# Attention, SwiGLU gate and output projection on one core: another place for the divided feed-forward tile, and another rule for the order of score copies

## The chip, the core and the metric

The kernel runs on one core of a Trainium2 chip. The time is device microseconds of one execution; the figure for a kernel is the median of several. A profiled execution also has a span, from its first to its last instruction, which is a little shorter than its time. The engines are PE (TensorE, matrix products), DVE (VectorE), ACT (ScalarE), POOL (GpSimd) and SP (which here only issues DMAs). They run side by side, each in the order of its own instructions, and wait for one another by semaphores.

## What is computed

One layer on a sequence of 2048 tokens of width 512, in fp32: a layer norm, full attention with 32 heads of 16, a SwiGLU feed-forward of width 1792 whose output gates the attention's output, and a residual.

```python
def _A_ref(x, wqkv, wo):                      # B, S, D = 1, 2048, 512; H = 32; Dh = 16
    q, k, v = ...                             # x @ wqkv, by heads
    scores = jnp.einsum("bhqd,bhkd->bhqk", q, k) * scale
    p = _softmax(scores, axis=-1)
    o = jnp.einsum("bhqk,bhkd->bhqd", p, v)
    return ... @ wo

def _B_ref(x, w_gate, w_up, w_down):          # F = 1792
    g = _silu(x @ w_gate)
    u = x @ w_up
    return (g * u) @ w_down

xn = _layernorm(x, axis=-1)
s = _A_ref(xn, A_wqkv, A_wo)
g = _silu(_B_ref(xn, B_w_gate, B_w_up, B_w_down))
return x + s * g
```

## The kernel before

**Two kinds of work side by side.** After a first stage (layer norm, projections) comes one long stage in which attention and feed-forward are mixed by hand. Nothing is scheduled by the compiler (`manual_schedule`): the order of the Python calls is the order on each engine.

**Attention** is cut into 32 *units*: eight groups of four heads by four stretches of 512 queries. A unit goes through 16 key tiles of 128 keys, in three *blocks* (96 in all; here they are counted from 0, so unit u has blocks 3u to 3u+2). `blocks` holds unit, first key tile and number n of key tiles; `run` issues one block. Each key tile gives two *pairs* of heads. For a pair, PE makes two score products of 128 by 512 at once, one in the upper and one in the lower 64 rows of its array, and ACT takes the exponential of both.

- A **direct pair** (`"D"`, function `scored`) uses one of two PSUM score tiles in turn; ACT reads it straight from PSUM (L954). The next but one direct pair needs that exponential done.
- A **copied pair** goes through a single spare PSUM bank (`acc[1]`) in two *halves*: `"A"` makes the first product and DVE copies it to SBUF (L1010), `"B"` the second (L1016). Each half needs the copy before it done, since there is only one bank. ACT takes the exponentials of the copied pairs at the end of the block (L1024). A half uses only one half of the array's rows; `lower` turns the order of the next products round, so that the other half of the rows is not idle.

After a block's scores come its **value products** (`values`, L409): per key tile four products in four column strips of the array, written as two instructions each, 8 instructions per key tile in all. They need the exponentials.

**Feed-forward** is a stream of *products* (`"F"`, one call of `fill(1)`; `both`, L187): two matrix products at once, into the PSUM tiles bankx (upper rows) and banky (lower rows). For each of four token blocks and two groups of seven feature tiles there are seven *gate and up tiles* of 24 products each and then four *down tiles* of 21 products each. At the end of a gate and up tile ACT takes a tanh (L239) and DVE makes two products (L240, L241) and two splits into high and low parts; at the end of a down tile DVE adds both banks to an accumulator. Work for DVE that may come later is put into `chores`, with a cost in units of a product, and `run` places chores between copies where `events` leaves room; `tidy` places all that is left.

**How they are matched.** `sizes` holds the number of products for each block: normally one tile per block. There are 87 tiles left at the start and 88 blocks before the tail (`early = 88`), so one tile must be divided over two blocks. Blocks 88 to 95 take the products of the output projection (18, 24, 24, 24, 12, 12, 24, 24; L380, `project_out`), which halfway through each tile turns the two banks round after DVE has read one element of each (`turned_over`, L384).

- A unit normally has n of 5, 5 and 6, with the 6 where a block has most products. Units with a divided tile have 6, 6, 4 and then 4, 6, 6, so that the blocks with half a tile have 4 key tiles.
- `begins` lists blocks whose first two direct pairs are made early: `begin` issues them in the block before, ahead of that block's last key tile of value products. In `events` such a block has `ahead` set to 2.
- `events(n, f, ahead)` sets the order within a block. It gives each direct pair and each copied half a time in units of a product (direct pairs at 0, 1 and then from 7 on some 4 to 5 apart, halves from 2.2 on some 5.6 to 8 apart), sorts them, and fills the room with products. Where the times are crowded they are issued in the order of the list, as close as they come.

From the names in `order`'s rows: acc_80 is `acc[0]` (value products), acc_81 the spare bank, score_8970 and score_8971 the two score tiles.

Of the kernel before, what the change touches and what calls it, by code (L numbers as in the profile page):

```python
# [21 lines left out]
D = 512  # L22
H = 32
DH = 16
F = 1792
# [14 lines left out]
DC = D // HALF  # L40
# [3 lines left out]
EPS = 1e-5  # L44
TURNS = (0, 0, 0, 0, 0, 2, 4, 6, 8, 10, 13, 16, 16)
COPIES = ((0, 0, 0, 1, 1, 1, 1, 0, 0, 0, 0, 2), (1, 1, 0, 0, 1, 1, 1, 1, 2, 2, 0, 0))
QSLOT = (0, 1, 0)
KSLOT = (0, 0, 1)

# [2 lines left out]
def tile_block(ctx: ExitStack, tc: tile.TileContext, x, wqkv, wo, w_gate, w_up, w_down, out):  # L52
    nc = tc.nc
    ctx.enter_context(tc.manual_schedule())
    x, out = x[0], out[0]
# [39 lines left out]
    def load_rows(dst, src, slots):  # L95
        for h in range(2):
            for s, part in enumerate(slots):
                r = h * HALF + 2 + s * DH
                sp.dma_start(dst[r:r + DH].bitcast(F32),
                             src[part].rearrange("(j h d) t -> h d j t", j=2, h=2)[h])  # L100
# [5 lines left out]
    def load_q(u, i=None):  # L106
        g, b = divmod(u, NB)
        load_rows(qst[u % 2 if i is None else i], q_d[:, g * 64:(g + 1) * 64, b * TB:(b + 1) * TB], QSLOT)

# [353 lines left out]
    units = NG * NB  # L463
# [19 lines left out]
    sizes = []  # L483
    for _ in range(NB):
        for part in GROUPS:
            nf = part.stop - part.start
            sizes += [3 * DC] * nf + [3 * nf] * NT
    split = sizes[-1] // 2
    sizes = sizes[1:-1] + [sizes[-1] - split, split]
    early = len(sizes)  # L490
    pair = 6 * DT
    sizes += [6 * (DT - 1), pair, pair, pair, pair // 2, pair // 2, pair, pair]
    begins = (early - 2, early - 1, early, early + 4, early + 5)

    blocks, opened = [], []
    for u in range(units):
        opened.append(len(blocks))
        if u == 0:
            ns = [4, 6, 6]
        elif u >= units - 4:  # L500
            ns = ([4, 6, 6] if u % 2 else [6, 6, 4])
        else:
            ns = [5] * 3
            far = sizes[len(blocks):len(blocks) + 3]
            ns[far.index(max(far)) if far[1] < max(far) else 1] = 6
        kt = 0
        for n in ns:
            blocks.append((u, kt, n))
            kt += n

    def events(n, f, ahead):
        length = 2 * n - ahead + f
        need = 2 * n - max(2, (10 * length + 46) // 40)
        fit = (10 * length + 55) // 112
        copied = n - 3 if ahead else max(0, min(need, fit)) if now else 0
        direct = 2 * n - copied
        gap = max(4, min(5, (length - 8) / max(1, direct - 2)))
        marks = [] if ahead else [(0, "D"), (1, "D")]
        marks += [((0.5 if ahead else 7) + gap * i, "D") for i in range(direct - 2)]
        marks += [((0.3 if ahead else 2.2) + max(5.6, min(8, (length - 5) / (2 * copied))) * i, "AB"[i % 2]) for i in range(2 * copied)]  # L520
        marks.sort(key=lambda mark: mark[0] - 0.6 * (mark[1] == "D"))
        out = []
        at = left = 0
        for t, kind in marks:
            while left < f - (kind != "D") and at < t:
                out.append((at, "F"))
                left += 1
                at += 1
            out.append((at, kind))
            at += 1 if kind == "D" else 0.5  # L530
        return direct, out + [(at + i, "F") for i in range(f - left)]

    with ExitStack() as pro:
        pc = pro.enter_context(tc.tile_pool(name="pc", bufs=1))
# [118 lines left out]
        def split_x(b, t, av, between=None):  # L653
            hi, lo = (xt[b % 2][j][:, :, t * P:(t + 1) * P] for j in range(2))
            nc.scalar.copy(hi, av)
            if between:
                between()
            dve.tensor_sub(lo, av, hi.bitcast(F32))
# [119 lines left out]
        def copy_fx(i):  # L778
            i, w = divmod(i, 2)
            i, u = divmod(i, 2)  # L780
            j, h = divmod(i, 2)
            dst = fx[halves[h], j].rearrange("p (c u) t -> u p c t", u=2)[u]
            nc.scalar.copy(dst[:, 2 * w:2 * w + 2], xt[0][j][halves[u], 2 * w:2 * w + 2])

        copied = list(range(16))
# [11 lines left out]
        for b in range(NB):  # L797
# [3 lines left out]
            for n, (make, i) in enumerate(slots):  # L801
# [27 lines left out]
                if b == 0 and n == 2:  # L829
                    split_x(0, 0, xf)  # L830
                for _ in range(COPIES[b][n] if b < 2 else 0):
                    copy_fx(copied.pop(0))
# [57 lines left out]
        with tc.If(fast < 1):  # L890
            with tc.tile_pool(name="gen", bufs=1) as gen:
                for h in range(2):
                    pool.memset(qst[0][h * HALF:h * HALF + 2].bitcast(F32), 0.0)
                for g in range(NG):
                    for b in range(NB):
                        u = g * NB + b
                        load_q(u, 0)
                        mx = gen.tile([P, 4 * NT, 4], F32, tag="mx", name="mx")
                        for j in range(NB):
                            load_k(g, j, j % 2)  # L900
                            for i in range(4 * NT):
                                h, t = divmod(i, NT)
# [60 lines left out]
    def run(u, first, n):  # L963
        nonlocal lower
        f = sizes.pop(0) if sizes else 0
        direct, todo = events(n, f, len(begun))
        if now == 0:
            for _ in range(4):
# [172 lines left out]
```

## Time and profile before

| | |
|---|---|
| time, median of 3 runs | 1397.09 us (1396.32 to 1397.9) |
| time of the profiled execution | 1397.09 us |
| its span | 1395.3 us, granted TensorE clock 0.999 |
| value products (L409) | 4096 instructions |
| direct pairs (L954) | 860 exponentials |
| copied pairs (L1010, L1016, L1024) | 164 |
| DVE busy | 755.9 us of the span |

The main view is the chain of work that ended last, in order of time. It follows the program back from its last instruction, at each step to what released it or to the instruction before it on its engine. A row gives start, length and the work. In the long stage nearly all of it is PE, so a block can be read off between two of its runs of value products: a row `x40` is the value products of a block with 5 key tiles, `x48` of one with 6, `x32` of one with 4; where the next block is begun early the last key tile has a row `x8` of its own. The end of such a run (start plus length) is the end of the block.

The other views used are the timeline (instructions of an engine in order of time, with the wait ahead of them in brackets and its releaser) and the page's tables of engines and of groups of instructions.

### The profile page before, as it was taken

What the parts mean: (1) busy time and instruction counts of PE and PEld (TensorE: products, weight loads), DVE (VectorE), ACT (ScalarE), POOL (GpSimd) and SP (SyncE); (2) the same over time, 40 slices, a digit from 0 to 9 for tenths busy, and PEclk for the clock granted to TensorE, in tenths of its full rate; (3) what the DMA queues carried; (4) which work ended last, traced back from release to release, by engine and by line L of the source; (5) the groups of instructions that cost most, each with busy time, mean ns of one, the idle gap of its engine ahead of it and who ended that gap; (6) DMA issues with size and microseconds to landing.
All of it is one profiled execution on the core that took longest, in us unless ns stands there. A gap on an engine that the chain in (4) does not pass through costs nothing.

```text
span 1395.3 us, 27643 instructions
## 1 busy us (share of the span) xinstructions
PE 1387.7 (99%) x11193; PEld 849.8 (61%) x11193; DVE 755.9 (54%) x1293; ACT 1087.4 (78%) x1245; POOL 73.7 (5%) x92
## 2 busy tenths in 40 slices
PE   9999999999999999999999999999999999999998
PEld 7777755655665565565556556655655665564555
DVE  6674555455645653556456645654565445555544
ACT  6753678877888877787888778778877877889785
POOL 4200200000000000000000000000000000000222
PEclk9999999999999999999999999999999999999999
DMA  7778641043534511154514303256134113234323
GB/s 228 271 246 267 173 107 43 14 115 85 130 86 118 119 43 36 51 132 97 136 53 110 97 13 73 74 141 149 57 76 114 32 47 80 63 92 141 116 86 137
DMA packets 126953, 148.13 MB, mean 106 GB/s; under 512 B 12524, under 2 KB 79340, under 8 KB 126052
## 3 DMA queue, kind: packets, MB, share of 16 engines
q1 hardware_dynamic: 121620, 125.79, 34.8%
q0 software_dynamic: 4912, 20.12, 3.9%
q8 instruction: 89, 1.46, 0.4%
q14 instruction: 44, 0.36, 0.1%
q10 hardware_dynamic: 288, 0.39, 0.1%
HBM read 106.68 MB, written 39.58 MB: 105 GB/s over the span
## 4 chain that ended last, share of the span: by engine, by line
PE 88%; ACT 0%; DVE 0%; issue 0%; DVEq 0%
PE acc L409 32%; PE bankx L187 23%; PE score L948 17%; PE banky L187 10%; PE acc L948 3%; PE bankx L380 2%; PE banky L380 1%; ACT pr L954 0%; PE acc L1078 0%; PE bankx L1078 0%; PE score L1078 0%; DVE pr L1010 0%; DVE y L1085 0%; DVE pr L1016 0%; DVE fx L1022 0%
## 5 line engine op out<-in xcount | busy, mean ns | idle before, releaser
L954 ACT ACTIVATE pr<-score 128x1024 f32<-128x1024 f32 x860 | 813.4, 1032 | 226.2 <-PE score L948 224.5
L409 PE MATMUL acc<-pr,vst 128*17 128x512 f32 x4096 | 459.1, 593 | 0.0
L948 PE MATMUL score<-qst,kst 50*128 50x512 f32 x1720 | 395.4, 412 | 0.1
L187 PE MATMUL bankx<-fx,guh 64*128 64x512 f32 x896 | 333.5, 393 | 0.1
L187 PE MATMUL banky<-fx,guh 64*128 64x512 f32 x896 | 324.9, 393 | 0.0
L409 PEld LDWEIGHTS acc<-pr,vst 128*17 128x17 f32 x4096 | 109.9, 97 | 290.6 <-issue 270.9
L948 PEld LDWEIGHTS score<-qst,kst 50*128 50x128 f32 x1720 | 176.3, 184 | 142.5 <-issue 66.3
L1010 DVE COPY pr<-acc 128x512 f32<-128x512 f32 x164 | 113.3, 691 | 188.1 <-PE acc L948 186.0
L187 PE MATMUL bankx<-wd,hh 64*128 64x512 f32 x672 | 201.2, 392 | 0.0
L187 PE MATMUL banky<-wd,hh 64*128 64x512 f32 x672 | 198.8, 393 | 0.0
L187 PEld LDWEIGHTS bankx<-fx,guh 64*128 64x128 f32 x896 | 166.6, 186 | 18.4 <-issue 0.9
L187 PE MATMUL banky<-fx,gul 64*128 64x512 f32 x448 | 175.6, 392 | 0.0
L187 PE MATMUL bankx<-fx,gul 64*128 64x512 f32 x448 | 175.4, 392 | 0.0
L187 PEld LDWEIGHTS banky<-fx,guh 64*128 64x128 f32 x896 | 166.5, 186 | 5.5
L1024 ACT ACTIVATE pr<-pr 128x1024 f32<-128x1024 f32 x164 | 168.0, 1078 | 0.0
L1016 DVE COPY pr<-acc 128x512 f32<-128x512 f32 x164 | 113.3, 691 | 74.9 <-PE acc L948 65.9
L240 DVE SCALAR_TENSOR_TENSOR ga<-th,bankx 128x512 f32<-128x512 f32 x56 | 38.5, 688 | 177.9 <-ACT th L239 177.9
L187 PEld LDWEIGHTS bankx<-wd,hh 64*128 64x128 f32 x672 | 124.9, 186 | 14.2 <-DVE fx L1022 0.8
L948 PE MATMUL acc<-qst,kst 50*128 50x512 f32 x328 | 131.9, 402 | 0.1
L187 PEld LDWEIGHTS banky<-wd,hh 64*128 64x128 f32 x672 | 124.5, 186 | 3.5
L187 PEld LDWEIGHTS bankx<-fx,gul 64*128 64x128 f32 x448 | 83.7, 187 | 9.9
L187 PEld LDWEIGHTS banky<-fx,gul 64*128 64x128 f32 x448 | 83.6, 186 | 3.2
(186 smaller groups left out, 1296.3 us busy)
## 6 DMA issues: line engine op xcount, KB each, us to landing
gur<-in_B_w_gate_dram SPq DMA_DIRECT2D x56, 256.0 KB
gur<-in_B_w_up_dram SPq DMA_DIRECT2D x56, 256.0 KB
wdr<-in_B_w_down_dram SPq DMA_DIRECT2D x56, 256.0 KB
kst<-k_d SPq DMA_DIRECT2D x192, 64.0 KB
qst<-q_d SPq DMA_DIRECT2D x192, 64.0 KB
fx<-xt_d SPq DMA_DIRECT2D x24, 512.0 KB
q_d<-parts SPq DMA_DIRECT2D x16, 512.0 KB
k_d<-parts SPq DMA_DIRECT2D x16, 512.0 KB
```

What stands on the lines that cost most here:

```text
L187: mm(banks[i], lhs[halves[i]], rhs[halves[i]], start=start, stop=stop)
L240: dve.scalar_tensor_tensor(ga, th, 1.0, bankx, op0=ALU.add, op1=ALU.mult)
L380: mm(banks[k], lhs[b, c][a][halves[h], (j + k) * P:(j + k + 1) * P], fx[halves[h], w, c], start=swap == i == 0, stop=i == 3 * n - 1, skip_ ...
L409: mm(acc[0][h * 32:h * 32 + DH + 1], v[:, kt % CT, h * (DH + 1):(h + 1) * (DH + 1)], probs[kt, h // 2][:, h % 2], start=kt == 0, stop=kt = ...
L948: mm(bank, k[r, j, kc * P:(kc + 1) * P], qst[u % 2][r, j], start=True, stop=True)
L954: act(pr, score[slot], AF.Exp, scale=0.25)
L1010: dve.tensor_copy(probs[kt, j][:, 0], spare_bank)
L1016: dve.tensor_copy(probs[kt, j][:, 1], spare_bank)
L1024: act(probs[kt, j], probs[kt, j], AF.Exp, scale=0.25)
```

## The change

Two things change, both in the tables that set the order.

**Which tile is divided.** Before, the last down tile was divided, 11 and 10 products in blocks 86 and 87. Now that is one tile in block 87, and the gate and up tile that blocks 68 and 69 (units 22 and 23) share is divided, 12 and 12 products. All tiles between move by one block. Units 22 and 23 get 6, 6, 4 and 4, 6, 6 key tiles, units 28 and 29 go back to 5, 5 and 6. Blocks begun early were 86, 87, 88, 92 and 93; now they are 68, 69, 92 and 93. Key tiles / products by block:

| block | 66 | 67 | 68 | 69 | 70 | 71 | 72 | 73 | 74, 75 | 76 | 77 | 78 to 82 |
|---|---|---|---|---|---|---|---|---|---|---|---|---|
| before | 5/24 | 6/24 | 5/24 | 5/24 | 6/24 | 5/24 | 5/21 | 6/21 | 5/21 | 6/24 | 5/24 | - |
| now | 6/24 | 6/24 | 4/12 | 4/12 | 6/24 | 6/24 | 6/24 | 5/21 | 5/21 | 5/21 | 6/24 | as before |

| block | 83 | 84 | 85 | 86 | 87 | 88 | 89 on |
|---|---|---|---|---|---|---|---|
| before | 5/21 | 6/21 | 6/21 | 4/11 | 4/10 | 6/18 | - |
| now | 5/24 | 5/21 | 6/21 | 5/21 | 5/21 | 5/18 | as before |

**The order within a block.** `events` now walks through time: a direct pair is issued as soon as its time has come, a copied half only when its time has come and five products have passed since the half before it; a direct pair that is due within 0.6 goes first. Of the kinds of blocks that stay, this alters only those with 6 key tiles and 21 products and no early begin: blocks 7, 19, 40 and 52, and 85 in both kernels. There the first half of the third copied pair comes one product later and the second half one direct pair later. In all there are 859 direct and 165 copied pairs now.

On PE, the middle of block 52, from the second half of the second copied pair to the first half of the third (bankx and banky are the feed-forward, score_8970 a direct pair, acc_81 a copied half). Before:

```order
L948 MATMUL acc_81<-qst_8987,kst_8979 128x512
L187 MATMUL bankx<-wd,hh 128x512
L187 MATMUL banky<-wd,hh 128x512
L187 MATMUL bankx<-wd,hh 128x512
L187 MATMUL banky<-wd,hh 128x512
L948 MATMUL score_8970<-qst_8987,kst_8979 128x512 x2
L187 MATMUL bankx<-wd,hh 128x512
L187 MATMUL banky<-wd,hh 128x512
L948 MATMUL acc_81<-qst_8987,kst_8979 128x512
```

Now (lines are 1 to 12 higher in the changed file):

```order
L960 MATMUL acc_81<-qst_8987,kst_8979 128x512
L188 MATMUL bankx<-wd,hh 128x512
L188 MATMUL banky<-wd,hh 128x512
L188 MATMUL bankx<-wd,hh 128x512
L188 MATMUL banky<-wd,hh 128x512
L960 MATMUL score_8970<-qst_8987,kst_8979 128x512 x2
L188 MATMUL bankx<-wd,hh 128x512
L188 MATMUL banky<-wd,hh 128x512
L188 MATMUL bankx<-wd,hh 128x512
L188 MATMUL banky<-wd,hh 128x512
L960 MATMUL acc_81<-qst_8987,kst_8979 128x512
```

One more product (a row of bankx and one of banky) stands between the two halves: five in place of four, the direct pair counted as one.

On DVE, block 88, from the first half of the first copied pair on. Before (L1022 is a chore, L384 the reads after which the projection's banks turn round):

```order
L1010 COPY pr<-acc_81 128x512
L1016 COPY pr<-acc_81 128x512
L1022 TENSOR_TENSOR fx<-wor,fx 128x512
L1010 COPY pr<-acc_81 128x512
L384 COPY turned_over<-bankx 1x1
L384 COPY turned_over<-banky 1x1
L1016 COPY pr<-acc_81 128x512
```

Now, from the chore on:

```order
L1034 TENSOR_TENSOR fx<-wor,fx 128x512
L1022 COPY pr<-acc_81 128x512
L1028 COPY pr<-acc_81 128x512
L385 COPY turned_over<-bankx 1x1
L385 COPY turned_over<-banky 1x1
L1022 COPY pr<-acc_81 128x512
```

The two small reads stood behind the first half of the second copied pair and now stand ahead of it; the chore stands ahead of both halves of the first pair.

On DVE, block 69 now, from the chores that block 68 leaves (the divided tile's splits, `guh`, `gul` and `wd`) to the tile's end; nothing there stood so close before, since block 69 was a whole tile:

```order
L1034 TENSOR_TENSOR gul<-gur,guh 128x512
L1034 CAST wd<-wdr 128x512
L1034 TENSOR_TENSOR wd<-wdr,wd 128x512
L421 STREAM_TRANSPOSE o<-acc_80 128x512
L426 RECIPROCAL rl<-o 128x16
L1022 COPY pr<-acc_81 128x512
L430 TENSOR_TENSOR on_8997<-o,rl 128x16x16
L1028 COPY pr<-acc_81 128x512
L446 STREAM_TRANSPOSE o<-on_8997 128x512
L241 SCALAR_TENSOR_TENSOR ga<-th,bankx 128x512
L242 SCALAR_TENSOR_TENSOR ga<-ga,banky 128x512
```

The transposition of acc_80 (the result of unit 22) has to be done before block 69's value products overwrite it; the splits of the divided tile are ahead of it in the queue.

```diff
+PARTED = (22, 23)
...
-    split = sizes[-1] // 2
-    sizes = sizes[1:-1] + [sizes[-1] - split, split]
+    sizes = sizes[1:]
+    sizes[3 * PARTED[0] + 2:3 * PARTED[1]] = [3 * DC // 2] * 2
     early = len(sizes)
     pair = 6 * DT
     sizes += [6 * (DT - 1), pair, pair, pair, pair // 2, pair // 2, pair, pair]
-    begins = (early - 2, early - 1, early, early + 4, early + 5)
+    begins = tuple(3 * u + i for a in (PARTED[0], units - 2) for u, i in ((a, 2), (a + 1, 0)))
...
-        elif u >= units - 4:
+        elif u in PARTED or u >= units - 2:
             ns = ([4, 6, 6] if u % 2 else [6, 6, 4])
...
         gap = max(4, min(5, (length - 8) / max(1, direct - 2)))
-        marks = [] if ahead else [(0, "D"), (1, "D")]
-        marks += [((0.5 if ahead else 7) + gap * i, "D") for i in range(direct - 2)]
-        marks += [((0.3 if ahead else 2.2) + max(5.6, min(8, (length - 5) / (2 * copied))) * i, "AB"[i % 2]) for i in range(2 * copied)]
-        marks.sort(key=lambda mark: mark[0] - 0.6 * (mark[1] == "D"))
+        far = max(5.6, min(8, (length - 5) / max(1, 2 * copied)))
+        ds = [] if ahead else [0, 1]
+        ds += [(0.5 if ahead else 7) + gap * i for i in range(direct - 2)]
+        cs = [((0.3 if ahead else 2.2) + far * i, "AB"[i % 2]) for i in range(2 * copied)]
         out = []
-        at = left = 0
-        for t, kind in marks:
-            while left < f - (kind != "D") and at < t:
+        at, free = 0, 0
+        while f or ds or cs:
+            d = bool(ds) and at >= ds[0]
+            c = bool(cs) and at >= max(cs[0][0], free)
+            spare = f > bool(cs)
+            if d and c:
+                d = ds[0] - 0.6 <= cs[0][0]
+            if d or not c and not spare and ds:
+                out.append((at, "D"))
+                ds.pop(0)
+                at += 1
+            elif c or not spare and cs:
+                out.append((at, cs.pop(0)[1]))
+                at += 0.5
+                free = at + 5
+            else:
                 out.append((at, "F"))
-                left += 1
+                f -= 1
                 at += 1
-            out.append((at, kind))
-            at += 1 if kind == "D" else 0.5
-        return direct, out + [(at + i, "F") for i in range(f - left)]
+        return direct, out
```

## The prediction

> **What bounds the kernel now.** I read the page's table of engines first, then its chain of waits, then the same chain in order of time.
>
> ```profile
> PE 1387.7 (99%) x11193; PEld 849.8 (61%) x11193; DVE 755.9 (54%) x1293; ACT 1087.4 (78%) x1245; POOL 73.7 (5%) x92
> ...
> PE 88%; ACT 0%; DVE 0%; issue 0%; DVEq 0%
> ```
>
> PE is busy for 99% of the span and holds nearly all of the chain; ACT has a fifth of the span free. So time is gained or lost only in how closely PE's work is packed. The 99% can't show that, since a product that starts late still counts as busy beside its neighbour. What shows it is the length of a block, read between the ends of two runs of value products in the chain in order of time (start, length; a run's end is their sum). These are the ends of blocks 65 to 68, 72 to 75, 77, 81 and 82:
>
> ```profile
> 997.59 5.27 PE acc L409 x48
> 1011.06 4.42 PE acc L409 x40
> 1024.15 5.27 PE acc L409 x48
> 1037.60 4.42 PE acc L409 x40
> ...
> 1088.78 4.42 PE acc L409 x40
> 1101.57 5.28 PE acc L409 x48
> 1114.35 4.42 PE acc L409 x40
> 1126.29 4.42 PE acc L409 x40
> ...
> 1152.88 4.42 PE acc L409 x40
> ...
> 1204.78 4.41 PE acc L409 x40
> 1217.91 5.29 PE acc L409 x48
> ```
>
> and these the ends of blocks 83 to 89 and 91 to 93 (an `x8` is the last key tile of a block whose follower is begun early):
>
> ```profile
> 1230.66 4.42 PE acc L409 x40
> 1243.31 5.28 PE acc L409 x48
> 1256.81 4.42 PE acc L409 x40
> 1261.88 0.98 PE acc L409 x8
> 1267.42 2.70 PE acc L409 x24
> 1270.78 0.98 PE acc L409 x8
> 1276.37 2.70 PE acc L409 x24
> 1279.74 0.98 PE acc L409 x8
> 1289.00 5.28 PE acc L409 x48
> ...
> 1303.18 5.27 PE acc L409 x48
> ...
> 1331.66 4.42 PE acc L409 x40
> 1336.74 0.98 PE acc L409 x8
> 1342.31 2.70 PE acc L409 x24
> 1345.67 0.98 PE acc L409 x8
> 1351.24 3.56 PE acc L409 x32
> ```
>
> **Prices of blocks**, as key tiles/products. 5/24: block 68, 1042.02 - 1029.42 = 12.60; block 66, 1015.48 - 1002.86 = 12.62; I take 12.61. 6/24: block 67, 13.94, and block 82, 1223.20 - 1209.19 = 14.01; I take 13.97. 5/21: block 74, 1118.77 - 1106.85 = 11.92, and block 75, 11.94; I take 11.93. So a product costs (12.61 - 11.93)/3 = 0.23 and a key tile 13.97 - 12.61 = 1.36. By these 6/21 should cost 13.97 - 0.69 = 13.28, but block 84 takes 1248.59 - 1235.08 = 13.51 and block 73 13.65: this kind of block loses 0.2 to 0.4 us inside. A block that begins its follower early pays for it: in block 91 the value products last from 1331.66 to 1337.72, 6.06 in place of 5.27, so 0.79 more. The two half blocks behind it, 4/12 each, take 1346.65 - 1337.72 = 8.93 (it begins the next one too) and 1354.80 - 1346.65 = 8.15.
>
> The part that is undone, blocks 85 to 88, takes 14.27, 8.90, 8.96 and 13.56. Content doesn't explain the last: 6/18 by the prices is 13.97 - 6 x 0.23 = 12.59, less the two pairs that block 87 has made for it, two products or 0.46, so 12.13. Block 88 loses 1.4 us. The chain names it:
>
> ```profile
> 1282.93 0.69 DVE pr L1016
> 1283.62 0.60 DVE fx L1022
> 1284.22 0.68 DVE pr L1010
> 1284.90 0.13 DVE turned_over L384 x2
> ```
>
> Four DVE instructions in a row hold PE from 1282.93 to 1285.03: the small reads that let the projection's banks turn round stand in DVE's queue behind a copy that itself had to wait.
>
> **The change part by part.**
>
> *Blocks 66 to 73* (now 6/24, 6/24 with a begin, 4/12 with a begin, 4/12, three of 6/24, 5/21). Before: 1106.85 - 1002.86 = 103.99. Now: 13.97 + (13.97 + 0.79) + 8.93 + (8.15 + 0.1) + 3 x 13.97 + 11.93 = 99.75. The 0.1 is the one thing that blocks 92 and 93, the model of the pair, don't have: a gate and up tile ends with a tanh on ACT. What it takes from ACT is seen in block 43, where the next exponential starts 0.48 after it:
>
> ```profile
> 715.84 0.63 ACT L239 ACTIVATE th<-bankx 128x512 f32<-128x512 f32 x1
> 716.32 1.07 ACT L954 ACTIVATE pr<-score 128x1024 f32<-128x1024 f32 x1
> ...
> 1352.26 1.05 ACT L1024 ACTIVATE pr<-pr 128x1024 f32<-128x1024 f32 x1
> ```
>
> The last row is the copied pair's exponential in block 93: it ends at 1353.31, and the last of four key tiles needs it at about 1351.24 + 3/4 x 3.56 = 1353.9 at the latest. 0.48 later it ends at 1353.79, so the cover of 0.6 shrinks to 0.1. Bounds: nothing, or the whole 0.48; I take 0.1, near the first, for the semaphore. DVE's part of the tile (three splits of guh and gul, two of wd) falls into block 68; how much cover it has there is told with the third rival. Behind the tanh on ACT stands one direct pair's exponential, for which the same key tile waits, and on DVE the two products of the tile, needed only by the tile after. Change: -4.24. Most of that isn't gain: these blocks now hold 21 products fewer, which turn up below.
>
> *Blocks 76 and 77*: before 1157.30 - 1130.71 = 26.59, now 11.93 + 13.97 = 25.90: -0.69, three products fewer.
>
> *Blocks 83 to 88*: before 1294.28 - 1223.20 = 71.08. Now 12.61 + 11.93 + 6/21 + 11.93 + 11.93 + block 88. The loads of the output projection's weights and of its left operand move by one block together with the tiles that they follow, and the order on SP between them is kept, so I cost them at nothing; were they late, the next projection block would wait.
>
> *Block 88* becomes 5/18 without an early begin: 11.93 - 3 x 0.23 = 11.24 if nothing stalls. On DVE the small reads now stand ahead of the second copied pair, and the chore ahead of the first, which ends about 8.5 x 0.23 + 0.42 + 0.69 = 3.1 us into the block (8.5 products stand ahead of its second half; 0.42 and 0.69 are a half's latency and copy, rows below), before the feed-forward's ninth product is done (13 products in, 3.0, and 0.42). What stays is the turn itself, which block 89 shows: it has the same order around it and takes 1308.45 - 1294.28 = 14.17, 0.20 over a 6/24. So 11.45; bounds 11.24 and 11.24 + 1.4 = 12.6, the old stall whole. I take 11.45, by the nearest row.
>
> *6/21 by the new rule.* In block 19 the third copied pair waits for the copy ahead of it:
>
> ```profile
> 404.09 0.38 PE L948 MATMUL acc<-qst,kst 50*128 50x512 f32 x1
> ...
> 404.51 0.69 DVE L1016 COPY pr<-acc 128x512 f32<-128x512 f32 x1 [0.82 <-PE acc L948]
> ...
> 405.26 0.18 PEld L948 LDWEIGHTS acc<-qst,kst 50*128 50x128 f32 x1 [0.28 <-DVE pr L1016]
> ```
>
> The half's product starts at 404.09, its copy 0.42 later and ends at 405.20, and the weights of the next half are loaded at 405.26, the moment the bank is free. So halves can't follow each other faster than about 0.42 + 0.69 + 0.06 = 1.17. Four products and the half's own 0.12 are 4 x 0.23 + 0.12 = 1.04: some 0.12 is lost. Five products are 1.27 and lose nothing there. One of the three such places is mended, so I take 0.11 off per block (bounds 0 and the whole 0.23 that block 84 loses): 13.51 - 0.11 = 13.40 for block 85, and 4 x 0.11 = 0.44 for blocks 7, 19, 40 and 52.
>
> So blocks 83 to 88: 12.61 + 11.93 + 13.40 + 11.93 + 11.93 + 11.45 = 73.25, +2.17 (24 products more, 5.5 us of work, for 2.2 us).
>
> **Sum**: -4.24 - 0.69 + 2.17 - 0.44 = -3.2. The uncertain terms (0.1, 0.2, 5 x 0.11) lean to a smaller gain, so I round to -3.1. The span of 1395.3 becomes 1392.2; the profiled execution's own time is 1397.09, which is also the median of the three runs: 1397.09 - 3.1 = **1394.0 us**, a gain of 0.22%.
>
> **The rivals.**
>
> *The turn's stall stays.* If the small reads in block 88 still wait, because the chore or the first pair is late, its 1.4 comes back less the 0.2 already counted: -3.1 + 1.2 = -1.9, 1395.2. For it: the queue on DVE has the same pieces. Against it: their order, and block 89.
>
> *Only a begin fewer.* Products, key tiles and value products are the same in both kernels, and 164 or 165 copied pairs make no difference. If the losses of blocks 85 to 88 lay only in the early begins, five becoming four would give 0.79 - 0.46 = 0.33: 1396.8. The Trainium skill, page "TensorEngine Tiling (Array Packing)", section "Tiling Modes", says that a change of the tiling mode drains the engine, and an early begin costs two such changes more. The trace agrees that a begin costs 0.33 too much, but blocks 86 to 88 show stalls on top, with rows of their own.
>
> *Vector work piles up in the half blocks* (the slower side). Place: the second copied half of block 69, which waits on DVE for the first copy, and this for the transposition of unit 22's result, ahead of which stand the splits of the divided tile. Block 87 of before has the same head of a unit:
>
> ```profile
> 1272.81 0.63 DVE L1010 COPY pr<-acc 128x512 f32<-128x512 f32 x1
> ...
> L1022 DVE TENSOR_TENSOR gul<-gur,guh 128x512 fp32r<-128x512 f32 x108 | 72.4, 683 | 0.3
> ```
>
> There the first copy, with the transposition ahead of it, ends at 1273.44, 1.68 after the block's start at 1271.76; in block 69 the second half is due after 7.5 products, 1.73. So from a backlog of 0.1 us on PE waits, microsecond for microsecond. If all nine DVE instructions of a gate and up tile, at most 0.69 each, stood there, PE would lose 6.2: 1394.0 + 6.2 = 1400.2; slower than before from a backlog of 3.1 on. Against it: the five splits, some 3.4, begin at the head of block 68, which lasts 8.93 and holds only two copies (1.4) beside them; the other four belong to the tile's end.
>
> *More comes back*: block 88 without any turn wait and 0.2 from each 6/21 block, another 0.7: 1393.3.
>
> **How the numbers follow.** About 0.2% (2.8 us) is what a measurement of this kernel can tell from no change, so the line lies at 1394.3, close to the forecast. Chances: the forecast 0.68 (its own range 1393.2 to 1395.0; four fifths of it faster by over 0.2%), the turn's stall 0.10, only a begin 0.05, piled up vector work 0.08, more 0.09. Faster 0.54 + 0.09 = 0.63; within 0.2%: 0.14 + 0.10 + 0.05 + 0.01 = 0.30; slower 0.07. For 8 in 10 the range takes in the stall's case and the larger gain: 1392.9 to 1396.0.
>
> **What would show it.** In the chain of the new profile: blocks 68 and 69 at 8.9 and 8.2 (if 69 is over 9, vector work piled up); block 88 at 11.4 to 11.6 with no run of DVE instructions in the chain (over 12.5: the stall stayed); 6/21 blocks at 13.4 to 13.5 (13.6: the spacing did nothing); plain blocks as before. If plain blocks change their length, the prices were not portable and the prediction is wrong for a reason that it doesn't name.

## The result, and the profile after

| | before | changed |
|---|---|---|
| median of 11 runs, us | 1397.04 (1396.32 to 1397.9) | 1393.65 (1393.53 to 1394.52) |
| profiled execution, us | 1397.09 | 1393.85 |
| its span, us | 1395.3 | 1392.1 |
| ratio of the medians | | 0.9976, interval 0.9968 to 0.9984 |

The change makes the kernel 3.4 us faster, 0.24%; 1394.0 was predicted. These are the page's table of engines and the shares of the chain of waits by engine, of the changed kernel:

```profile
PE 1386.0 (100%) x11193; PEld 850.6 (61%) x11193; DVE 757.7 (54%) x1295; ACT 1087.5 (78%) x1245; POOL 74.4 (5%) x92
...
PE 88%; ACT 0%; DVE 0%; issue 0%; DVEq 0%
```

As many matmuls as before, no engine noticeably busier: the page can't tell where 3.2 us of span went. The chain in order of time can (start, length, what). These are the value products that end blocks 65 to 73, and then 83 to 88, of the changed kernel (L410 is the L409 of before):

```profile
997.42 5.27 PE acc L410 x48
1011.39 5.27 PE acc L410 x48
1025.36 4.42 PE acc L410 x40
1030.44 0.98 PE acc L410 x8
1035.95 2.70 PE acc L410 x24
1039.31 0.99 PE acc L410 x8
1044.88 3.63 PE acc L410 x32
1057.19 5.27 PE acc L410 x48
1071.15 5.27 PE acc L410 x48
1085.11 5.28 PE acc L410 x48
1097.92 4.42 PE acc L410 x40
...
1226.06 4.42 PE acc L410 x40
1238.01 4.42 PE acc L410 x40
1250.57 5.28 PE acc L410 x48
1263.35 4.42 PE acc L410 x40
1275.26 4.42 PE acc L410 x40
1286.69 4.42 PE acc L410 x40
```

Ends subtracted from ends give the blocks. The two that share the divided tile are at 1040.30 - 1031.42 = 8.88 (block 68) and 1048.51 - 1040.30 = 8.21 (block 69); block 85 is 1255.85 - 1242.43 = 13.42, and block 88 is 1291.11 - 1279.68 = 11.43. No DVE row stands among these in the chain any more.

| blocks | before | predicted | measured | gain or loss |
|---|---|---|---|---|
| 66 to 73 | 103.99 | 99.75 | 99.65 | -4.34 |
| 76, 77 | 26.59 | 25.90 | 25.89 | -0.70 |
| 83 to 88 | 71.08 | 73.25 | 73.25 | +2.17 |
| 7, 19, 40, 52 | 54.30 | 53.86 | 53.82 | -0.48 |

Together -3.35. The other blocks from 1 on differ by no more than 0.12 each and are 0.2 shorter in all, while block 0 ends 0.3 later than before (166.71 against 166.40), a difference that the prediction doesn't have; in the kernels below that end varies by as much, from 166.4 to 167.1. The profiled execution took 1393.85, and the prediction's unrounded sum was 1397.09 - 3.2 = 1393.89. So the gain is won where it was put: eight blocks give up 21 products and get shorter by 4.34, three products leave blocks 76 and 77, and blocks 83 to 88 take the 24 products and get longer by only 2.17, since their own losses are gone.

That the transposition in block 69 isn't late is read from DVE's timeline of the changed kernel (start, length, what; in brackets the idle time before it and who ended it):

```profile
1035.31 0.69 DVE L1034 TENSOR_TENSOR wd<-wdr,wd 128x512 fp32r<-128x512 f32 x1
1040.42 0.72 DVE L421 STREAM_TRANSPOSE o<-acc 128x512 f32<-128x512 f32 x1 [4.42 <-PE acc L410]
1041.34 0.65 DVE L1022 COPY pr<-acc 128x512 f32<-128x512 f32 x1
```

The last split ends at 1036.00, and DVE then waits 4.42 for PE: that much vector work more would fit there. And this is ACT's timeline at the end of block 69:

```profile
1044.97 0.59 ACT L240 ACTIVATE th<-bankx 128x512 f32<-128x512 f32 x1
1045.45 1.03 ACT L966 ACTIVATE pr<-score 128x1024 f32<-128x1024 f32 x1
1046.35 1.07 ACT L1036 ACTIVATE pr<-pr 128x1024 f32<-128x1024 f32 x1
```

The tile's tanh stands ahead of the last two exponentials. The last ends at 1047.42; the last of four key tiles, three quarters into the run that starts at 1044.88, needs it at 1044.88 + 3/4 x 3.63 = 1047.60. The cover is 0.18.

### The profile page after: what moved, and what is told of

The parts are those of the page before. It is cut to its first block, busy times and chain, and to the rows that moved or that the text cites. A ratio compares the mean times of both kernels' runs of the same rounds, so it can differ in the third digit from the quotient of the medians.

```text
span 1392.1 us, 27644 instructions
## 1 busy us (share of the span) xinstructions
PE 1386.0 (100%) x11193; PEld 850.6 (61%) x11193; DVE 757.7 (54%) x1295; ACT 1087.5 (78%) x1245; POOL 74.4 (5%) x92
## 4 chain that ended last, share of the span: by engine, by line
PE 88%; ACT 0%; DVE 0%; issue 0%; DVEq 0%
PE acc L410 32%; PE bankx L188 23%; PE score L960 17%; PE banky L188 10%; PE acc L960 3%; PE bankx L381 2%; PE banky L381 1%; ACT pr L966 0%; PE acc L1090 0%; PE bankx L1090 0%; PE score L1090 0%; DVE y L1097 0%; DVE y L1103 0%; DVEq L1149 0%
## 5 line engine op out<-in xcount | busy, mean ns | idle before, releaser
L410 PE MATMUL acc<-pr,vst 128*17 128x512 f32 x4096 | 459.0, 593 | 0.0
L410 PEld LDWEIGHTS acc<-pr,vst 128*17 128x17 f32 x4096 | 110.1, 97 | 290.8 <-issue 269.2
L1022 DVE COPY pr<-acc 128x512 f32<-128x512 f32 x165 | 114.1, 692 | 186.8 <-PE acc L960 183.8
L188 PEld LDWEIGHTS banky<-fx,guh 64*128 64x128 f32 x896 | 166.4, 186 | 5.2
```

Source lines behind the costliest of these rows:

```text
L188: mm(banks[i], lhs[halves[i]], rhs[halves[i]], start=start, stop=stop)
L410: mm(acc[0][h * 32:h * 32 + DH + 1], v[:, kt % CT, h * (DH + 1):(h + 1) * (DH + 1)], probs[kt, h // 2][:, h % 2], start=kt == 0, stop=kt = ...
L1022: dve.tensor_copy(probs[kt, j][:, 0], spare_bank)
```

## The experiments

Each kernel was timed in five rounds against the kernel before on the same chip (1397.24 to 1397.32 there); the ratios are to that. "My theory" in the expectations is that of the prediction: prices of blocks carry over, block 88's loss is DVE's queue, the place of the tile doesn't matter. Lengths of blocks come from one profiled execution of each kernel.

**The division alone.** The changed kernel with the old `events`, of which these lines decide where copied halves stand:

```diff
-                free = at + 5
...
+        marks.sort(key=lambda mark: mark[0] - 0.6 * (mark[1] == "D"))
```

> The change's division (gate and up tile of units 22 and 23, four early begins), with the order of before within each block. My theory: 1394.2, since the only blocks that differ from the changed kernel are the five of 6 key tiles and 21 products, which go back to 13.5 to 13.65 us each (0.11 more apiece); block 88 keeps its order and stays at 11.4. Rival, only the number of early begins counts: 1397.04 - 0.33 = 1396.7. Rival, the gain is all in the new order within the blocks: 1397.

Measured: 1394.49, ratio 0.9981 (0.9972 to 0.9990): -2.8. Block 88 stays at 11.43, and the 6/21 blocks go back: 7 from 13.50 to 13.67, 19 from 13.42 to 13.48, 40 from 13.42 to 13.51, 52 from 13.48 to 13.63, 85 from 13.42 to 13.49; 0.54 together. So beside the division the spacing carries only the 0.55 (5 x 0.11) that the sum gave it. The fence shows the wait itself, in block 19 of this kernel, as a row of PE's weight loads:

```profile
405.32 0.18 PEld L949 LDWEIGHTS acc<-qst,kst 50*128 50x128 f32 x1 [0.28 <-DVE pr L1017]
```

The weights for the next copied half wait 0.28 for the copy ahead of them, as in the row that the prediction showed. The changed kernel has the same load without a wait:

```profile
405.38 0.18 PEld L960 LDWEIGHTS acc<-qst,kst 50*128 50x128 f32 x1
```

**The spacing alone.** The kernel before with the new `events`, the same edit the other way round:

```diff
-        marks.sort(key=lambda mark: mark[0] - 0.6 * (mark[1] == "D"))
...
+                free = at + 5
```

> The kernel before with the change's order within blocks alone: division, units and five early begins as before. My theory: 1394.6. Seven blocks of 6 key tiles and 21 products lose 0.11 less each (0.8 in all); in blocks 86 and 87 five products stand between the two copied halves in place of four, 0.2 each; in block 88 the reads that turn the banks round now stand ahead of the second copied pair, so most of its 1.4 goes (1.2). Rival, the loss of blocks 85 to 88 lies in their early begins: only the 0.8, 1396.2.

Measured: 1395.78, ratio 0.9988 (0.9979 to 0.9997): -1.5, where the theory had -2.4 and the rival -0.8. Blocks 7, 19, 40, 52 and 73 win 0.07 to 0.20 each, but blocks 84 and 85, which were to win 0.11 each as well, only 0.02; why is not shown. Block 86 wins 0.09, block 87 0.25 and block 88 only 0.59 of its 1.4 (12.97), so the rival, by which these three win nothing, doesn't hold either. The chain of this kernel has the rest, at the end of block 88:

```profile
1285.79 0.70 DVE pr L1021
...
1287.27 5.27 PE acc L409 x48
```

The turn no longer holds PE, but a copied half does. The two parts alone make 2.83 + 1.54 = 4.37, together 3.39. The difference of about 1 is what both repair: 0.09 + 0.25 + 0.59 of blocks 86 to 88 and 0.15 of block 73, since 86 and 87 hold whole tiles and 88 and 73 have only 5 key tiles once the tile is divided elsewhere.

**Block 88's queue alone.** The kernel before, with one half moved behind one product, so that the small reads stand ahead of its copy on DVE:

```diff
+        if now == early:
+            half = [i for i, (_, e) in enumerate(todo) if e == "A"][1]
+            todo[half:half + 2] = todo[half + 1], todo[half]
```

> The kernel before with one instruction of block 88 moved on PE: the first half of the second copied pair comes behind the ninth product of the projection in place of ahead of it, so that on DVE the two small reads that turn the banks round are no longer queued behind its copy. My theory: block 88 falls from 13.56 to 12.3 to 12.5, the time to 1395.9. Rival, block 88 is slow because of its early begin or because ACT is behind: 13.5, 1397.0.

Measured: 1396.69, ratio 0.9996 (0.9987 to 1.0005); block 88 goes from 13.56 to 12.99. That is 0.57, not the 1.1 to 1.3 expected: the theory falls as to size. And the 0.57 is what remains after a loss, since the swap also brings the second pair's halves one product closer together, four apart in place of five. On DVE's timeline of this kernel the reads do stand ahead of the copy, and what is left is seen behind them:

```profile
1284.51 0.14 DVE L384 COPY turned_over<-banky 1x1 f32<-1x1 f32 x1
1284.59 0.67 DVE L1013 COPY pr<-acc 128x512 f32<-128x512 f32 x1
1285.85 0.69 DVE L1019 COPY pr<-acc 128x512 f32<-128x512 f32 x1 [0.59 <-PE acc L948]
1287.13 0.69 DVE L1013 COPY pr<-acc 128x512 f32<-128x512 f32 x1 [0.59 <-PE acc L948]
1288.41 0.69 DVE L1019 COPY pr<-acc 128x512 f32<-128x512 f32 x1 [0.59 <-PE acc L948]
```

Four copies at equal steps of 1.26 to 1.28, with the same 0.59 of idle time ahead of three of them: DVE waits for PE's half, and PE's next half for DVE's copy, in turn, with nothing to spare between them. A half can follow another here every 1.28 and not sooner; the prediction had estimated 1.17. It took the 0.42 of a half whose weights had been loaded early; in block 19 of the kernel before, the half whose load had to wait until 405.26 is copied from 405.79 on, 0.53 later.

That the third pair waits as well could have been read before any run. The chain of the kernel before has another DVE row in block 88, behind the four that the prediction showed:

```profile
1287.53 0.70 DVE pr L1010
```

It is the copy of the third pair's first half, for which the second half waits. In this kernel's chain the same copy stands from 1287.13 on.

**And the last pair moved apart.** The same kernel, with the third pair's halves five products apart in place of three:

```diff
+            for kind, places in (("A", -1), ("B", 1)):
+                half = [i for i, (_, e) in enumerate(todo) if e == kind][-1]
+                todo.insert(half + places, todo.pop(half))
```

> e4_swap, with the third copied pair of block 88 moved apart as well: its first half one product earlier, its second half behind the block's last product, so that five products lie between them in place of three. My theory now: what was left of block 88's loss after the swap is that pair, whose second half waits some 0.5 for DVE; block 88 from 12.99 to 12.5, the time 0.4 to 0.5 below e4_swap, 1.1 below the kernel before. Rival, the rest of the loss is the early begin or ACT: block 88 stays at 13.0.

Measured: 1396.38, ratio 0.9994 (0.9985 to 1.0003); block 88 at 12.75. It wins another 0.24, where 0.45 was expected. Of the block's 1.4, undoing DVE's queue thus wins 0.57 and moving the third pair 0.24; 0.2 or a little more is what every block with a turn in its middle has over its price. Some 0.4 is left, and its cause stays open. The first and the second pair's halves are still four products apart, and so now are the second and the third pair, which by a cycle of 1.28 can lose up to 1.28 - (4 x 0.23 + 0.12) = 0.24 at each place; the copies from 1284.88 on still follow each other by 1.26 to 1.28 here. But no DVE row is left in this block's part of the chain, and no run moved these halves.

**The turn without cover.** The changed kernel, without the step that moves a direct pair to the place where the projection's banks turn round:

```diff
-        if now >= early and f != pair // 2:
+        if now > len(blocks):
```

> The changed kernel without the direct pair that is moved to the place where the projection's banks turn round (six blocks: 88 to 91, 94, 95). My theory: the turn takes a fixed time of which that pair covers one product, so each of these blocks loses 0.2 to 0.25 more, 1.2 to 1.5 in all. Rival, the 0.2 that these blocks lose lies in the moved pair itself (ACT idle before it): 1.2 faster than the changed kernel.

Measured: 1395.16, ratio 0.9985 (0.9976 to 0.9994), that is -2.1 in place of -3.4, so 1.3 slower than the changed kernel. Blocks 88, 89, 90, 91, 94 and 95 are each 0.23 to 0.27 longer, about one product (0.23). The view of `turned_over` agrees: PE's weight loads wait for the small reads six times here, 2.7 us in all, and only twice, 0.3 in all, in the changed kernel. So the turn makes PE wait and the moved pair covers most of that. That the 0.20 by which block 89 still exceeds a plain 6/24 is the rest of this wait is likely, but not shown.

**Without the early begins at the new place.**

```diff
-    begins = tuple(3 * u + i for a in (PARTED[0], units - 2) for u, i in ((a, 2), (a + 1, 0)))
+    begins = (early + 4, early + 5)
```

> The changed kernel without the early begins of blocks 68 and 69 (those of 92 and 93 stay); both half blocks then have 6 direct and 2 copied pairs. Rival, a begin is only a cost of 0.33 us for the array's change of tiling: 1393.65 - 0.66 = 1393.0. My theory: without the head start ACT is late, since in 20 products (4.7 us) it can't get through 6 exponentials at 0.93 and the copied pairs' two, and the last key tile's value products wait 0.5 in block 68 and 1.0 in block 69, where the tanh comes on top: 1393.65 + 0.6 = 1394.3.

Measured: 1394.77, ratio 0.9983 (0.9974 to 0.9992): 0.8 slower than with them, by medians whose intervals overlap. The blocks tell it clearly: block 67 wins 0.81 (14.76 to 13.95), and blocks 68 and 69 lose 0.33 and 1.52 (to 9.21 and 9.73); in all 1.0 longer, where 0.6 was expected. ACT's timeline of this kernel at the end of block 69 shows why:

```profile
1044.10 1.94 ACT L966 ACTIVATE pr<-score 128x1024 f32<-128x1024 f32 x2
1045.93 0.60 ACT L240 ACTIVATE th<-bankx 128x512 f32<-128x512 f32 x1
1046.41 2.02 ACT L1036 ACTIVATE pr<-pr 128x1024 f32<-128x1024 f32 x2
```

The last exponential ends at 1048.43, and the last key tile's value products, which end the block at 1049.5, can't start before. Block 69's eight exponentials and the tanh keep ACT busy from 1040.34 to 1048.43 without a pause, 8.1 us, as long as the half block itself: without work done ahead ACT is the bound there. So a begin isn't only a loss: here the two cost 0.8 in block 67 and save 1.9 in blocks 68 and 69. That fits the fall of the rival "only a begin fewer", which already falls by its size: 0.33 where 3.4 was measured for the whole change and 2.8 for the division alone.

**The tile at another place, and of another kind.** First a gate and up tile four units earlier, then a down tile six units earlier, in parts of 11 and 10 products.

```diff
-PARTED = (22, 23)
+PARTED = (18, 19)
```

```diff
-PARTED = (22, 23)
+PARTED = (16, 17)
...
-    sizes[3 * PARTED[0] + 2:3 * PARTED[1]] = [3 * DC // 2] * 2
+    sizes[3 * PARTED[0] + 2:3 * PARTED[1]] = [11, 10]
```

> The changed kernel with the gate and up tile of units 18 and 19 divided in place of that of units 22 and 23. My theory: it only matters that the divided tile lies among gate and up tiles away from the projection; by the prices of blocks this has one more block of 6 key tiles and 21 products, so 0.2 slower than the changed kernel: 3.2 below the kernel before. Rival, the place at units 22 and 23 was worth something by itself (what runs beside it, loads): over 1 slower than the changed kernel.

> The changed kernel with a down tile divided, 11 and 10 products in units 16 and 17, in place of the gate and up tile. My theory: what was wrong before was not the kind of tile but the crowded block 88 behind it; by the prices of blocks, two more blocks of 6 key tiles and 21 products, 0.3 slower than the changed kernel, so 3.1 below the kernel before. Rival, a divided down tile is worse by itself, because 10 products are too few to cover 7 exponentials and a copied pair: blocks 50 and 51 at 8.9 and 8.9 as blocks 86 and 87 were, 1 slower than the changed kernel.

Measured: 1394.20, ratio 0.9978 (0.9969 to 0.9987), and 1394.45, ratio 0.9979 (0.9970 to 0.9988): -3.1 and -2.9, neither told apart from the changed kernel. In the first, the chain has the same three blocks at the new place:

```profile
857.48 5.28 PE acc L410 x48
871.46 4.42 PE acc L410 x40
876.53 0.98 PE acc L410 x8
882.02 2.70 PE acc L410 x24
885.39 0.98 PE acc L410 x8
890.95 3.62 PE acc L410 x32
```

877.51 - 862.76 = 14.75, 886.37 - 877.51 = 8.86 and 894.57 - 886.37 = 8.20, beside 14.76, 8.88 and 8.21. In the second, these rows of the chain end the blocks 49 to 51:

```profile
800.33 0.98 PE acc L410 x8
...
809.00 0.98 PE acc L410 x8
814.38 3.56 PE acc L410 x32
```

Blocks 50 and 51 take 809.98 - 801.31 = 8.67 and 817.94 - 809.98 = 7.96, not the 8.9 and 8.9 of the rival. In the kernel before, the same two halves took 8.90 and 8.96; 0.79 of the second is the early begin of block 88, so some 0.2 each was lost by their place and the order within them.

**Vector work ahead of the transposition.** The changed kernel with one of the subtractions that block 68 does ahead of it, which only rewrites what it has written, repeated 5, 12 and, later, 9 times:

```diff
+                    if i == 45:
+                        chores.extend([chores[-1]] * 5)
```

> The changed kernel with the last split of block 68 on DVE made five times more (the same values written again), 3.0 us of extra DVE work ahead of the transposition of unit 22's result. In the changed kernel's trace DVE stands idle for 4.4 us there. My theory: all covered, the changed kernel's time within 0.2. Rival, DVE was what held the two half blocks: 3 slower.

> The same with twelve more, 7.3 us. My theory: 4.4 are covered, the rest of 2.9 comes back microsecond for microsecond, since the second copied half of block 69 stands right behind: the changed kernel's time + 2.8, all of it in blocks 68 and 69. Rival, the wait is taken up by slack elsewhere in block 69: under + 1.

> The changed kernel with nine more of the splits of block 68 on DVE. In e7_vector12 twelve took 0.725 us each, PE then waited 3.9 us, and lost 1.75 more because its clock had fallen to 0.63 in the four microseconds after. Here 9 x 0.725 = 6.5 less the 4.4 of cover: PE should wait 1.7 to 2.1. My theory: with so short a wait the clock stays at 1.00, and block 69 takes 8.2 + 1.9 = 10.1, no more. Rival, the extra loss in e7_vector12 has nothing to do with the clock (exponentials bunched behind the wait): a loss of some 3.0.

| repeats | us | ratio (interval) | block 69 |
|---|---|---|---|
| 0 | 1393.65 | 0.9976 (0.9968 to 0.9984) | 8.21 |
| 5 | 1393.80 | 0.9973 (0.9963 to 0.9983) | 8.20 |
| 9 | 1397.40 | 0.9998 (0.9989 to 1.0007) | 11.69 |
| 12 | 1400.64 | 1.0021 (1.0012 to 1.0030) | 13.84 |

Five are free, as the 4.42 of idle time said. Nine cost 3.5 in the block where 1.9 was expected, twelve 5.6 where 2.8 was. By the medians, each beside the kernel before, twelve cost even 6.7: the profiled execution, 1399.61, is one of the fastest of its eleven. Two things were missing from the expectation for twelve, and the second from that for nine as well. The repeats follow each other by 0.73 and not 0.6, probably because each waits for the one before; the chain of the kernel with nine has them:

```profile
1039.98 0.70 DVE gul L1036
...
1040.71 0.69 DVE gul L1036
1041.40 0.35 DVE wd L1036
...
1042.38 0.72 DVE o L423
...
1043.29 0.64 DVE pr L1024
```

These hold the second copied half, as the third rival said. But PE stands still only for 1.68, and this is what follows, in PE's timeline and in the view by windows (stretch, its length, busy time of PE, PEld, DVE, ACT and POOL with counts, then the granted clock, DMA share and GB/s) of the same kernel:

```profile
1043.98 0.71 PE L962 MATMUL acc<-qst,kst 50*128 50x512 f32 x1 [1.68 <-DVE pr L1024]
```

```profile
1042.00:1044.00 2.00, 0.32 (x5) 0.03 (x2) 1.97 (x5) 0.94 (x2) 0.00 (x0) 1.00 0.05 16
1044.10:1045.00 0.90, 0.90 (x6) 0.71 (x8) 0.42 (x2) 0.00 (x0) 0.00 (x0) 0.50 0.89 339
...
1046.00:1047.00 1.00, 1.00 (x6) 0.77 (x6) 0.04 (x1) 0.66 (x1) 0.54 (x1) 0.50 0.67 201
1047.00:1048.00 1.00, 1.00 (x9) 0.72 (x5) 0.00 (x0) 0.65 (x1) 0.00 (x0) 0.75 0.63 254
```

The granted clock is 1.00 through the wait, and 0.50 as soon as PE works again, until about 1047.5. 3.5 us at half the clock lose 1.75, and 1.68 + 1.75 = 3.43 is nearly the whole 3.48 that the block takes longer. After the longer wait with twelve repeats the clock falls too:

```profile
1042.00:1046.00 4.00, 0.13 (x3) 0.01 (x2) 3.90 (x8) 0.77 (x1) 0.00 (x0) 1.00 0.13 23
1046.00:1050.00 4.00, 4.00 (x21) 2.85 (x21) 1.58 (x3) 2.41 (x3) 0.54 (x1) 0.63 0.76 211
```

3.87 of 4.00 us idle, then a mean clock of 0.63: 1.5 lost in these 4 us. But not at once: taken by single microseconds, the clock is still 1.00 from 1046 to 1047, the first in which PE works again, and 0.50 to 0.51 from 1047 to 1050. So both expectations of the run with nine fell, the one that a short wait leaves the clock alone and the one that the clock has no part in it.

## Why the prediction was right

**Prices of blocks.** Right, and the reason that the sum was: every block of the three stretches came within 0.05 of its price, the half blocks at 8.88 and 8.21 too (8.93 and 8.25 predicted, after the model of blocks 92 and 93). The division moved by four units gives the same three lengths there. The down tile's halves, 8.67 and 7.96, are shorter than the 8.88 and 8.21 by 0.21 and 0.25, for one and two products less (0.23 and 0.46): the second is 0.2 over its price.

**The half blocks' cover on ACT.** Predicted as 0.1 left after the tanh, with 0.1 lost; measured as 0.18 left, and block 69 (8.21) is 0.06 over the 8.15 of its model, block 93; with cover left, what these 0.06 are is open. The eight blocks came 0.10 shorter than predicted, spread over most of them; and the uncertain terms did not lean to a smaller gain, for which the sum was rounded down by 0.1.

**Block 88.** Its length was right (11.45, measured 11.43), its loss of before was put to the wrong place in part. The step "Four DVE instructions in a row hold PE" gave the whole 1.4 to DVE's queue at the turn, and passed over the chain's row for the third pair. The runs give 0.57 to the queue, 0.24 to the third pair's halves, and 0.2 or so is still there in the changed kernel; the rest was not split further. It did no harm to the sum, which is luck as far as this step goes: the block's other crowding went as well when it became 5/18. It would have, had only the queue been mended: then 0.6 to 0.8 of the gain forecast for it would not have come.

**6/21 by the new rule.** Right in size (0.44 for four blocks, measured 0.48; with 85 0.54 by the first experiment), but the working behind it is not borne out. The cycle is 1.28 rather than 1.17, by which the mended place alone would lose 1.28 - 1.04 = 0.24 and not 0.12. Single blocks gain 0.06 to 0.17, and with the spacing alone blocks 84 and 85 hardly any: the 0.11 fits the mean, and that it does is in part luck.

**The rivals.** The turn's stall did not stay; the one early begin fewer explains only a tenth of the gain; the vector work did not pile up, with 4.4 us to spare where the prediction could only say that the splits begin early. In that rival the price "microsecond for microsecond" was wrong: beyond the cover nine repeats cost twice what PE waited in the profiled execution, because of the clock. Its 1400.2 for a backlog of 6.2 was therefore probably too low a price, not too high.

**Overlap.** What the prediction did not say is that its two parts repair partly the same thing: 2.8 and 1.5 alone, 3.4 together.

## What to carry to other kernels

On an engine that is 99% busy, read the lengths of equal pieces of work and not shares: a piece that costs more than its content names the place, and the prices of the others tell what moving work there is worth. Work that one bank serves in turn has a cycle of its own, here 1.28 us of matmul, copy and next load, and where a schedule asks for it sooner, both engines wait. Room in a queue is a number (here 4.4 us of DVE): below it added work is free, above it costs more than it lasts if PE, once it has stood still, is granted less clock.

## What the hardware showed that was not expected

A wait of 1.68 us on PE was enough for the granted clock to be 0.50 during the 3.5 us that followed. The Trainium skill, page "TensorE: Matmul & The Clock Gate", section "HAM oscillation — how this bites in real kernels", gives the rule as "no PE-idle gaps >~3.4µs.", the length of one window of the gate: the length at half clock, about 3.5 here, agrees, the gap from which it starts doesn't, since here half of that was enough. It isn't so in every run either: the spans of the eleven runs with nine repeats fall into 1393.9 to 1394.2 (four runs) and 1395.4 to 1396.9 (seven), about one such loss of 1.75 apart; the mean clock of their whole span is 0.999 to 1.000 in the four and 0.998 to 0.999 in the seven. The four lie 2.2 above the changed kernel's median span of 1391.8, near the 1.9 that was expected of a kept clock. But only a run of the upper group was profiled, so that the lower ones kept their clock is likely, not shown.

A DVE subtraction of 128x512 that writes the tile of the one before it starts 0.73 after it (the two rows of `gul` above), where instructions of that size that don't depend on each other can start 0.60 to 0.61 apart, though each is shown as about 0.69 long: in the changed kernel a copy starts at 1032.36 and the subtraction behind it at 1032.97, another subtraction at 1034.25 and the cast behind it at 1034.85.
